# A decode step of sliding-window attention plus a gated MLP: sixteen rows of wq are loaded once more, first in SyncE's queue

## The chip, the cores and the metric

The kernel runs on one core of one Trainium2 chip. The metric is the device time of one execution in microseconds, as the median of several runs. The profile is of one execution, with the instructions of the engines (TensorE, VectorE, ScalarE, GpSimd, and SyncE, called SP, which here only issues DMAs) and the packets that the core's 16 DMA engines moved.

## The reference: what is computed

One token for each of two sequences (B = 2, D = 512) is normalised, and two branches are added to it: attention with 32 query heads and 8 key/value heads of size 128 over the last 4096 positions of a cache, and a gated MLP with F = 1792.

```python
xn = _layernorm(x)                                   # x: (2, 1, 512)
q  = (xn @ wq)                                       # wq: (512, 4096), 32 heads of 128
k, v = k_cache[:, :, -4096:, :], v_cache[:, :, -4096:, :]    # each head repeated for 4 query heads
p  = softmax(q k^T * 128 ** -0.5)
a  = (p v) @ wo                                      # wo: (4096, 512)
gate, up = xn @ W_gate, xn @ W_up                    # (512, 1792) each
b  = (gate * (gate > 0) * up) @ W_down               # (1792, 512)
return x + a + b
```

All numbers are float32. About 95 MB of weights and cache are read, each byte once, for very little arithmetic.

## The kernel before, in words

All large inputs pass through one SBUF tile, `ring`, of four slots of 128 partitions x 8192 floats (4 MB). `place` (line 74) hands out the slots in turn. wq takes two slots (64 KB for each partition), W_gate one, W_up one; then come the cache pieces (`load_kv`, line 98), one slot each, in four groups g of two k pieces and two v pieces; then W_down and the two halves of wo.

The DMAs are issued from two queues. ScalarE's (ACT) takes the loads of wq, W_gate and W_up (`load_rows`, line 79) at the very start, one behind the other and with no wait. SP's takes the input x in three pieces (line 121), and then all cache pieces, W_down (line 95) and wo (line 463), each of which waits until the slot that it writes has been read by TensorE or VectorE. Each DMA counts up one of eight counters (shown as DMAHW0 to DMAHW7), which are given out in turn.

The order in time is the order of the code: the schedule is written by hand. At the start GpSimd and VectorE make constants. VectorE waits for x, makes its statistics (line 187) and the normalised xn (line 204); TensorE turns it (line 208), VectorE copies it to `xnT` (line 213), and TensorE multiplies it with wq (line 221, `q_ps`). The heads are spread into `qz` (lines 229 to 250). Then come gate and up (line 258, `g_ps` and `u_ps`), their product `hh`, and `hT`.

Then each group g runs through `scores` (line 286), `maxima`, `softmax`, `turn`, `values` (line 351) and `gather`. In `scores` VectorE transposes a k piece in 32 x 32 blocks into tiles `kT` (line 294), which TensorE multiplies with `qz` (line 301). The kT tiles come from the pool `ktp`, which has three buffers of 128 partitions x 4096 floats, handed out in turn. The first kT tile is made once `hT` is written. At the end W_down and wo are multiplied with the hidden values and the heads (lines 438 to 445, tiles `y4` and `y_ps`), and ScalarE copies the sum and stores it (lines 476 and 477).

Of the kernel before, what the change touches and what calls it, by code (L numbers as in the profile page):

```python
# [9 lines left out]
F32 = mybir.dt.float32  # L10
# [10 lines left out]
def kernel(  # L21
# [12 lines left out]
    nc = tc.nc  # L34
    P = 128
# [5 lines left out]
    W = min(4096, max(256, SK // 4))  # L41
# [20 lines left out]
    ktp = ctx.enter_context(tc.tile_pool(name="ktp", bufs=3))  # L62
# [53 lines left out]
        return wo[r * rows:(r + 1) * rows, :].rearrange("(p j) e -> p j e", p=P)[:, j0:j1, :]  # L116


    x2 = const.tile([B, D], F32, name="x2")
    for c0, c1 in ((0, 256), (256, 384), (384, 512)):  # L120
        nc.sync.dma_start(x2[:, c0:c1], x[:, 0, c0:c1])
# [384 lines left out]
```

## Time and profile before

| | |
|---|---|
| median of 3 runs | 229.9 us (229.74 to 230.0) |
| span of the profiled execution (first to last instruction) | 228.1 us |
| median less span | 1.8 us |
| TensorE busy | 158.3 us (69%) |
| VectorE busy | 101.6 us (45%) |
| ScalarE, GpSimd busy | 8.6 us, 6.4 us |
| DMA, mean over the span | 95.03 MB at 417 GB/s |

For the profiled execution the profile holds the span; what lies outside it is not recorded, so its own time beyond the span is not known. In the rows of the timeline and of the groups, the number in brackets at the end is the time for which the engine sat idle before the instruction, and `<-` names what it waited for. SPq and ACTq are the sequencers that issue DMAs. A row of busy times by stretches has the stretch, its length, the busy time of PE, PEld (weight loads), VectorE, ScalarE and GpSimd with the number of instructions, the granted clock of TensorE, the busy share of the 16 DMA engines, and GB/s. There a packet is counted where it begins, with its whole length and bytes, so in a stretch shorter than a packet the share can be above 1 or 0.

### The profile page before, as it was taken

Reading aid. Unit: us, or ns where it says so; the run is one execution under the profiler, and the core shown is the slowest. Engines: PE = TensorE matmul, PEld = TensorE weight load, DVE = VectorE, ACT = ScalarE, POOL = GpSimd, SP = SyncE. Lnnn points to the kernel's source line nnn. Section 1 sums busy time; section 2 is a strip of 40 time slices with the busy share of each in tenths; the row PEclk is TensorE's granted clock in tenths of the full one; section 3 lists DMA queues with packets and bytes.
Section 4 is the critical chain, followed back from the end, with each engine's and each line's share of the span. In section 5 each row is a group of like instructions: output and inputs, shape, how many; then the busy total and the mean of one; then the engine's idle time right before and its main releaser. Section 6 shows DMA issues by size and latency. Waiting matters only on the chain.

```text
span 228.1 us, 2218 instructions
## 1 busy us (share of the span) xinstructions
PE 158.3 (69%) x952; PEld 52.2 (23%) x952; DVE 101.6 (45%) x120; ACT 8.6 (4%) x28; POOL 6.4 (3%) x24
## 2 busy tenths in 40 slices
PE   0011982937199767897857897857887785788974
PEld 0011231413022121222212221212241121122512
DVE  2040003212999312699722599922169972212000
ACT  0010012200000010000010000000000001000000
POOL 8100000000000000000000000000000000000000
PEclk9999997697559965999997999999999999589999
DMA  9898999999999999999999999999999999999991
GB/s 368 368 437 379 463 434 437 423 447 414 425 450 422 408 460 431 408 448 434 425 425 454 414 417 454 419 431 442 437 422 425 442 419 425 432 413 422 434 395 60
DMA packets 3784, 95.03 MB, mean 417 GB/s; under 512 B 430, under 2 KB 448, under 8 KB 704
## 3 DMA queue, kind: packets, MB, share of 16 engines
q1 hardware_dynamic: 3324, 79.17, 80.9%
q10 hardware_dynamic: 452, 15.74, 16.2%
q8 instruction: 7, 0.11, 0.2%
q14 instruction: 1, 0.01, 0.0%
HBM read 94.90 MB, written 0.00 MB: 416 GB/s over the span
## 4 chain that ended last, share of the span: by engine, by line
DMA 54%; DVE 23%; PE 16%; issue 5%; ACTq 1%; ACT 1%; DVEq 0%
DMA ring<-in_A_k_cache_dram 25%; DMA ring<-in_B_W_up_dram 21%; DVE kT L294 19%; DMA ring<-in_A_wo_dram 8%; PE o L358 4%; PE s L301 3%; PE pp L343 3%; PE u_ps L258 2%; PE y_ps L445 1%; DVE pt L345 1%; PE y L438 1%; DVE m L316 1%; DVE on L367 1%; PE ht_ps L274 0%; ACT p L337 0%
## 5 line engine op out<-in xcount | busy, mean ns | idle before, releaser
L294 DVE STREAM_TRANSPOSE kT<-ring 128x2048 f32<-128x2048 f32 x32 | 71.0, 2278 | 5.9 <-DMA ring<-in_A_k_cache_dram 5.9
L301 PE MATMUL s<-kT,qz 128*32 128x512 f32 x256 | 58.7, 635 | 14.8 <-DVE kT L294 14.7
L358 PE MATMUL o<-ring,pt 128*32 128x512 f32 x256 | 35.7, 658 | 4.8 <-DVE rl L349 4.8
L301 PEld LDWEIGHTS s<-kT,qz 128*32 128x32 f32 x256 | 13.8, 112 | 58.6 <-issue 34.0
L367 DVE TENSOR_TENSOR on<-o,mask 128x512 f32<-128x512 f32 x8 | 5.4, 680 | 23.1 <-PE o L358 23.1
L358 PEld LDWEIGHTS o<-ring,pt 128*32 128x32 f32 x256 | 10.0, 118 | 23.6 <-issue 18.4
L343 PE MATMUL pp<-p,perm 128*128 128x512 f32 x16 | 12.2, 908 | 4.5 <-ACT p L337 4.5
L208 PE MATMUL xt_ps<-rep,xn 2*128 2x32 f32 x8 | 2.0, 415 | 16.2 <-DVE xn L204 16.2
L221 PE MATMUL q_ps<-ring,xnT 128*32 128x512 f32 x64 | 9.0, 726 | 4.6 <-DMA ring<-in_A_wq_dram 4.6
L345 DVE STREAM_TRANSPOSE pt<-pp 128x1024 f32<-128x1024 f32 x4 | 5.0, 1250 | 16.0 <-PE pp L343 16.0
L373 PE MATMUL oa<-on,picks 128*16 128x512 f32 x16 | 8.3, 597 | 3.8 <-DVE on L367 3.8
L316 DVE TENSOR_REDUCE m<-s 128x1 f32<-128x512 f32 x4 | 2.8, 692 | 12.8 <-PE s L301 12.8
L337 ACT ACTIVATE p<-s,nm 128x512 f32<-128x512 f32 x4 | 2.7, 687 | 143.5 <-DVE nm L331 143.5
L258 PE MATMUL u_ps<-ring,xnT 128*32 128x448 f32 x32 | 4.9, 780 | 3.8 <-DMA ring<-in_B_W_up_dram 3.8
L236 DVE COPY qT<-qt 128x32 f32<-128x32 f32 x2 | 0.4, 192 | 15.2 <-PE qt L232 15.2
L248 DVE COPY qz<-rq 32x32 f32<-32x32 f32 x16 | 3.0, 187 | 7.1 <-ACT qz L248 7.1
L438 PE MATMUL y<-ring,oT 128*32 128x512 f32 x48 | 5.5, 594 | 0.8 <-DMA ring<-in_A_wo_dram 0.8
L309 PE MATMUL idle<-pt,ident 128*128 128x512 f32 x12 | 6.0, 618 | 0.0
L343 PEld LDWEIGHTS pp<-p,perm 128*128 128x128 f32 x16 | 3.8, 266 | 7.9 <-issue 4.3
L208 PEld LDWEIGHTS xt_ps<-rep,xn 2*128 2x128 f32 x8 | 1.9, 322 | 16.1 <-issue 16.1
L187 DVE BATCH_NORM_STATS2 stats<-x 2x6 f32<-2x512 f32 x1 | 0.7, 680 | 10.4 <-DMA x<-in_A_x_dram 10.4
L221 PEld LDWEIGHTS q_ps<-ring,xnT 128*32 128x32 f32 x64 | 2.5, 130 | 10.4 <-issue 10.4
(81 smaller groups left out, 73.9 us busy)
## 6 DMA issues: line engine op xcount, KB each, us to landing
ring<-in_A_k_cache_dram SPq DMA_DIRECT2D x8, 4096.0 KB, 22.2
ring<-in_A_v_cache_dram SPq DMA_DIRECT2D x8, 4096.0 KB, 22.2
ring<-in_A_wo_dram SPq DMA_DIRECT2D x3, 2048.0 KB
ring<-in_B_W_gate_dram ACTq DMA_DIRECT2D x1, 3584.0 KB, 30.0
ring<-in_B_W_up_dram ACTq DMA_DIRECT2D x1, 3584.0 KB
ring<-in_B_W_down_dram SPq DMA_DIRECT2D x1, 3584.0 KB, 28.8
ring<-in_A_wo_dram SPq DMA_DIRECT2D x1, 1280.0 KB, 20.1
ring<-in_A_wo_dram SPq DMA_DIRECT2D x1, 512.0 KB, 20.9
```

The costliest lines, as they stand in the source:

```text
L221: nc.tensor.matmul(q_ps[r][32 * c:32 * c + 32, :], xnT[:, kc, :], wqt[:, kc, n * 512:(n + 1) * 512], start=(kc == 0), stop=(kc == KC - 1),)
L258: nc.tensor.matmul(dst[32 * c:32 * c + 32, :], xnT[:, kc, :], wt[:, kc, c * MQ:(c + 1) * MQ], start=(kc == 0), stop=(kc == KC - 1),)
L294: nc.vector.transpose(kt[:, lo:lo + JH // 2].rearrange("p j c k h -> p (j c k h)"), kt_in[:, j * DH:(j + JH // 2) * DH],)
L301: nc.tensor.matmul(ss[g][lo:lo + 32, :], qz[:, g, cb, h, 16 * a:16 * a + 32], kt[:, :, cb, :, h], start=(a == 0 and cb == 0), stop=(a == N ...
L309: nc.tensor.matmul(idle, ident, pts[g][:, 2 * n:2 * n + 2].rearrange("p n j k -> p (n j k)"), start=True, stop=True)
L316: nc.vector.tensor_reduce(out=m, in_=ss[g], op=ALU.max, axis=AX.X)
L343: nc.tensor.matmul(pp[:, h], perm[:, h], p, start=True, stop=True)
L345: nc.vector.transpose(pts[g].rearrange("p n j k -> p j n k"), pp.rearrange("p h y -> p y h"))
L358: nc.tensor.matmul(o[32 * q:32 * q + 32, :], pts[g][:, a * S1 + s1, j:j + 4, :].rearrange("p u k -> p (u k)"), v[:, lo:lo + 512], start=(s ...
L367: nc.vector.tensor_tensor(ons[a], os[a].rearrange("p (u d) -> p u d", u=4), mask[:, :, None].to_broadcast([P, 4, P]), op=ALU.mult)
L373: nc.tensor.matmul(oa[g], picks[:, a].rearrange("p h a i -> p (h a i)"), ons[a], start=(a == 0), stop=(a == NP - 1))
L438: nc.tensor.matmul(y4[32 * t:32 * t + 32, :], lhsT.rearrange("p b s -> p (b s)"), w, start=(i < Q), stop=(i >= EARLY - Q))
```

## The change

Two lines are added ahead of the load of x. A tile `few` is taken from the pool of the kT tiles (its first buffer, which no other tile uses until the transposes begin), and SP issues a DMA that loads rows 0 to 15 of wq, 4096 floats (16 KB) each, into the partitions 0, 7, 14, ..., 105 of it. Nothing reads them. All else is as it was; the kT tiles begin with the second buffer of their pool, the line numbers after it move by two, and the counters of the later DMAs by one.

```diff
@@ -116,6 +116,8 @@
         return wo[r * rows:(r + 1) * rows, :].rearrange("(p j) e -> p j e", p=P)[:, j0:j1, :]
 
 
+    few = ktp.tile([P, P * W // 128], F32, name="few", tag="kT")
+    nc.sync.dma_start(few[0:16 * 7:7, :], wq[0:16, :])
     x2 = const.tile([B, D], F32, name="x2")
     for c0, c1 in ((0, 256), (256, 384), (384, 512)):
         nc.sync.dma_start(x2[:, c0:c1], x[:, 0, c0:c1])
```

SP's list of the kernel before begins with the three pieces of x (two have one shape and share a row), then the cache pieces, with the counters that each waits for:

```order
L121 DMA x_76<-in_A_x_dram 2x256
L121 DMA x_76<-in_A_x_dram 2x128 x2
L106 DMA ring<-in_A_k_cache_dram 128x1x8192 [waits DMAHW0_49,PE_49]
L106 DMA ring<-in_A_k_cache_dram 128x1x8192 [waits PE_49]
L106 DMA ring<-in_A_v_cache_dram 128x1x8192 [waits DMAHW4_49,PE_49]
```

Of the changed kernel it begins so:

```order
L120 DMA few<-in_A_wq_dram 16x4096
L123 DMA x_78<-in_A_x_dram 2x256
L123 DMA x_78<-in_A_x_dram 2x128 x2
L106 DMA ring<-in_A_k_cache_dram 128x1x8192 [waits DMAHW0_49,PE_49]
L106 DMA ring<-in_A_k_cache_dram 128x1x8192 [waits PE_49]
L106 DMA ring<-in_A_v_cache_dram 128x1x8192 [waits DMAHW5_49,DMAHW1_49,PE_49]
```

The load of few has no wait and stands ahead of x. W_gate's counter has moved from DMAHW4 to DMAHW5, and few has taken DMAHW1, which the first v load uses again and so waits for.

VectorE's first transposes, group 0 (kT_a_s is the tile of k piece a and half s), before:

```order
L294 STREAM_TRANSPOSE kT_0_0_309<-ring 128x2048 [waits DMAHW5_49,DMAHW0_49]
L294 STREAM_TRANSPOSE kT_0_0_309<-ring 128x2048
L294 STREAM_TRANSPOSE kT_0_1_320<-ring 128x2048 x2
L294 STREAM_TRANSPOSE kT_1_0_331<-ring 128x2048 [waits DMAHW7_49]
L294 STREAM_TRANSPOSE kT_1_0_331<-ring 128x2048
```

And of the changed kernel:

```order
L296 STREAM_TRANSPOSE kT_0_0_311<-ring 128x2048 [waits DMAHW6_49,DMAHW0_49]
L296 STREAM_TRANSPOSE kT_0_0_311<-ring 128x2048
L296 STREAM_TRANSPOSE kT_0_1_322<-ring 128x2048 x2
L296 STREAM_TRANSPOSE kT_1_0_333<-ring 128x2048 [waits DMAHW1_49,DMAHW0_49]
L296 STREAM_TRANSPOSE kT_1_0_333<-ring 128x2048
```

The third tile, kT_1_0, takes the buffer that few had and waits for few's counter besides that of its k piece.

## The prediction

> **What bounds the kernel now.** I read the page's part 2 and part 3 first: is the DMA ever idle?
>
> ```profile
> span 228.1 us, 2218 instructions
> DMA  9898999999999999999999999999999999999991
> q1 hardware_dynamic: 3324, 79.17, 80.9%
> q10 hardware_dynamic: 452, 15.74, 16.2%
> ```
>
> The 16 DMA engines are busy from the second slice to the last but one; q1 (SP's queue) and q10 (ACT's) together fill 97.1% of their span. The busy time by stretches shows the same (the last two columns are DMA share and GB/s):
>
> ```profile
> 1.50:22.50 21.00, 2.04 (x8) 1.94 (x8) 3.62 (x13) 1.28 (x1) 5.52 (x18) 1.00 1.00 422
> 22.50:49.50 27.00, 17.98 (x120) 7.49 (x120) 4.70 (x20) 3.93 (x18) 0.00 (x0) 0.87 1.00 429
> 49.50:97.00 47.50, 35.34 (x194) 10.54 (x198) 25.85 (x23) 0.78 (x2) 0.00 (x0) 0.75 1.00 432
> 97.00:195.00 98.00, 77.18 (x392) 23.09 (x385) 62.52 (x54) 2.33 (x6) 0.00 (x0) 0.98 1.00 431
> 195.00:221.00 26.00, 22.40 (x168) 7.48 (x170) 4.00 (x8) 0.00 (x0) 0.00 (x0) 0.89 0.99 421
> 224.00:228.00 4.00, 1.23 (x36) 0.48 (x24) 0.00 (x0) 0.27 (x1) 0.00 (x0) 1.00 0.02 6
> ```
>
> The share is 0.99 to 1.00 in every stretch up to 221 us, while PE is below it in each (77.18 of 98.00 us in the longest). So the end is the start of the stream plus its bytes over its rate, plus a short tail. Does the tail hang on the last byte? The timeline there says so:
>
> ```profile
> 222.97 2.25 PE L445 MATMUL y_ps<-ring,oT 128*17 128x128 f32 x64
> 224.81 0.13 PEld L445 LDWEIGHTS y_ps<-ring,oT 128*17 128x17 f32 x8 [0.28 <-DMA ring<-in_A_wo_dram]
> 225.29 0.27 ACT L476 COPY yo<-y_ps 128x128 f32<-128x128 f32 x1 [32.20 <-PE y_ps L445]
> ```
>
> The last matmuls of y_ps still wait for wo, and the copy and the store follow at once. Whatever lengthens the stream lengthens the kernel; a delay on another engine costs nothing unless it lets the stream run dry.
>
> **The change, part by part.** It adds one DMA of 16 x 16 KB = 262,144 bytes, first in SP's queue. Priced as stream at the 429 to 432 GB/s of the rows above, that is 262,144 / 431,000 = **0.61 us**, if it is spread evenly (16,384 bytes for each engine) and nothing hides it. But it runs at the start, so the question is whether the engines were doing anything useful then. The issues at the start (start, duration), then what the engines began in each small stretch:
>
> ```profile
> 0.74 0.39 ACTq L81 DMA_DIRECT2D ring<-in_A_wq_dram  x1
> 0.74 0.94 SPq L121 DMA_DIRECT2D x<-in_A_x_dram  x3
> ```
>
> ```profile
> 1.50:2.00 0.50, 0.00 (x0) 0.00 (x0) 0.50 (x3) 0.00 (x0) 0.50 (x1) 1.00 3.62 1184
> 2.00:2.50 0.50, 0.00 (x0) 0.00 (x0) 0.47 (x2) 0.00 (x0) 0.50 (x1) 1.00 1.51 524
> 2.50:3.00 0.50, 0.00 (x0) 0.00 (x0) 0.00 (x0) 0.00 (x0) 0.50 (x2) 1.00 0.91 393
> 4.00:4.80 0.80, 0.00 (x0) 0.00 (x0) 0.00 (x0) 0.00 (x0) 0.74 (x4) 1.00 0.00 0
> 4.80:5.00 0.20, 0.00 (x0) 0.00 (x0) 0.00 (x0) 0.00 (x0) 0.20 (x2) 1.00 4.54 1969
> 5.00:5.20 0.20, 0.00 (x0) 0.00 (x0) 0.00 (x0) 0.00 (x0) 0.14 (x2) 1.00 4.54 1969
> 5.20:5.50 0.30, 0.00 (x0) 0.00 (x0) 0.00 (x0) 0.00 (x0) 0.24 (x3) 1.00 2.02 874
> 7.00:8.00 1.00, 0.00 (x0) 0.00 (x0) 0.00 (x0) 0.00 (x0) 0.00 (x0) 1.00 2.42 1049
> ```
>
> A share above 1 is a packet counted whole where it begins. wq is 128 rows of 64 KB, eight for each engine, so these are rounds of one row per engine. The round at 7 us takes 2.42 us, the second (4.54 x 0.20 + 4.54 x 0.20 + 2.02 x 0.30) also 2.42. The first, however, takes (3.62 + 1.51 + 0.91) x 0.50 = 3.02: its packets begin between 1.5 and 3.0 us but last 0.60 us longer. Six engines begin their second row in 4.80 to 5.00, six in 5.00 to 5.20, four in 5.20 to 5.50: on average at 5.09. Less 2.42, the first row flowed, in effect, from 2.67 on (2.4 to 3.1 by engine). And x's first pieces, issued at the same 0.74, were through long before:
>
> ```profile
> DMA packets 3, 0.00 MB, mean 15 GB/s; under 512 B 1, under 2 KB 3, under 8 KB 3
> q1 hardware_dynamic: 3, 0.00, 4.3%
> ```
>
> That is the stretch 1.60 to 1.74: three small packets of SP's queue, already moved. So from about 1.67 to 2.67 an engine could carry SP's packets without taking time from wq. few's packet needs 0.61 and ends at 2.28 if it begins where x's did.
>
> The bounds: 0 if it fits on every engine; 0.61 if wq's first row waits behind it and pays its 0.60 all the same. Below nothing there is a little room: if the slow beginning falls on few instead and wq flows from 2.28 on, 0.39 us are gained. The nearest rows (x's packets, same queue, same moment) lie at the low end, but they are two rows on two engines, and few's sixteen have to be set out before wq's; I take a third of the full price, **+0.2 us**.
>
> Next, the waits. In SP's list few stands ahead of x, and the first v load now waits for few's counter (DMAHW1) besides W_gate's; on VectorE the third kT tile takes few's buffer and waits for it besides the cache load. Both wait for a transfer of the first microseconds at instructions that stand behind the k loads of 28.44 us (row below). They cost nothing, and nobody queued behind them waits longer.
>
> x is another matter. Packets of SP's queue in 4.80 to 5.20 and in 12.00 to 12.40:
>
> ```profile
> DMA packets 14, 0.79 MB, mean 1969 GB/s; under 512 B 0, under 2 KB 2, under 8 KB 2
> q1 hardware_dynamic: 2, 0.00, 0.8%
> DMA packets 11, 0.59 MB, mean 1475 GB/s; under 512 B 2, under 2 KB 2, under 8 KB 2
> q1 hardware_dynamic: 2, 0.00, 0.3%
> ```
>
> Two data pieces (512 B) at the first place, two tiny completion writes at the second, one per engine: SP's queue gets one packet in, then a whole 64 KB row of wq, then the next. x's second and third pieces need data and completion each: four turns, which is why x lands after the fourth row. few's data and completion stand ahead, so the eight packets of an engine are one before the first row and seven turns: three more (few's data lasts 0.61, and wq's row is there before it ends), 3 x 2.42 = 7.26 us, up to 7.87 with few's own 0.61. The rows that this pushes:
>
> ```profile
> 12.83 0.68 DVE L187 BATCH_NORM_STATS2 stats<-x 2x6 f32<-2x512 f32 x1 [10.35 <-DMA x<-in_A_x_dram]
> 18.25 0.29 DVE L213 COPY xnT<-xt_ps 128x128 f32<-128x128 f32 x1 [2.23 <-PE xt_ps L208]
> 22.80 2.79 PE L221 MATMUL q_ps<-ring,xnT 128*32 128x512 f32 x12 [4.59 <-DMA ring<-in_A_wq_dram]
> 28.44 3.97 SPq L106 DMA_DIRECT2D ring<-in_A_k_cache_dram  x2
> 49.60 4.91 PE L258 MATMUL u_ps<-ring,xnT 128*32 128x448 f32 x32 [3.80 <-DMA ring<-in_B_W_up_dram]
> 93.20 5.83 SPq L106 DMA_DIRECT2D ring<-in_A_v_cache_dram  x2
> ```
>
> xnT is ready at 18.54 now, and PE starts at 22.80 on wq: 4.2 us of cover. After, xnT comes at 25.8 to 26.4, so q's matmuls start 3.1 to 3.6 us late. **That is hidden twice.** PE idles 3.80 us before u_ps for W_up, so it catches up there; with k's first load issued later (28.44 plus 3.1 to 3.6) gate and up have the engines to themselves for longer and land earlier. Meanwhile the stream has gate and up queued. Without the 3.80 the next cover is the queue. The sizes of the loads:
>
> ```profile
> ring<-in_A_k_cache_dram SPq DMA_DIRECT2D x8, 4096.0 KB, 22.2
> ring<-in_B_W_gate_dram ACTq DMA_DIRECT2D x1, 3584.0 KB, 30.0
> ring<-in_B_W_up_dram ACTq DMA_DIRECT2D x1, 3584.0 KB
> ```
>
> The cover is then this: the nine loads ahead of the v load issued at 93.20 are 39,936 KB (wq 8192, gate and up 3584 each, six cache loads of 4096), which the stretches above have moved by 97.0 (21 x 422 + 27 x 429 + 47.5 x 432 = 40.96 MB), so 3.8 us of work is still queued then.
>
> [...]
>
> Sum: +0.2 (few at the start) + 0 (waits) + 0 (x late, covered). Profiled span 228.1 to 228.3. The median shown, 229.9, stands 1.8 us above that span; I leave these outside parts as they are: **230.1 us**.
>
> **The rivals.**
>
> Paid in full: few's packets and wq's first rows share whatever made the first round slow, so nothing is hidden and the stream moves by 0.61: 229.9 + 0.6 = 230.5, slower. For it: most engines began their first row together (3.62 of the 6.04 in the first half microsecond), so the loss may be a contention that few joins. It decides from the point where few ends later than 2.4 + 0.46 on the engine that finishes last. Against: x's packets passed freely at that moment. Chance 0.28.
>
> [...] Chance 0.05.
>
> The stream runs dry: PE is late by more than 3.80 + 3.8, less the 0.93 from an issue (0.74) to its first packet (1.67), that is 6.7 us. Two turns more than I count would give 7.9 to 8.4 and a gap of 1.2 to 1.7: 231.1 to 231.6. For it: turns are long. Against: wq has only eight rows per engine, so there are hardly turns left. Chance 0.03, with an uneven spread of few's rows over the engines in it.
>
> The slow beginning is absorbed: wq flows from 2.28, -0.39, 229.5; still within 0.2%, and beyond it only if more than the mean is won. Chance 0.04 for faster.
>
> **How the numbers follow.** A difference under 0.2% (0.46 us) can't be told from none. Forecast, and the cases beside it that stay within 0.46 us: 0.60. Slower: 0.28 + 0.05 + 0.03 = 0.36. Faster: 0.04. The range is 229.5 (absorbed) to 230.9 (paid in full with some of the spread between engines); the doubled door and the dry stream are left out.
>
> **What would show it.** In the changed profile: x lands three turns later (stats at about 20.1 to 20.7); q's matmuls start at 25.9 to 26.4, waiting for xnT and no longer for wq; u_ps no longer waits for W_up but starts within 0.5 us of 49.6; the DMA share stays at 0.99 or 1.00 up to 221 us. The deciding row is the second round of wq: if it begins at 5.1 to 5.3 on average few was hidden, if at 5.7 it was paid. I am wrong if that round moves by over 0.46, or if a gap in the DMA share appears near 97 us.

## The result and the profile after

The changed kernel takes 231.18 us (median of 4 runs, 231.07 to 231.33) against 229.82 us before (4 runs): **1.36 us slower**, a ratio of 1.0055 with a 95% interval of 1.0036 to 1.0074. The prediction said 230.1, at most 230.9, and no measurable change as the likeliest case.

The page of the changed kernel, the same rows as before:

```profile
span 229.3 us, 2220 instructions
DMA  9988999999999999999999999999999999999991
q1 hardware_dynamic: 3356, 79.44, 80.8%
q10 hardware_dynamic: 452, 15.74, 16.4%
```

q1 has 32 packets more: sixteen rows of few and sixteen completions. The span grew by 1.2 us. The stream is as full as it was, and the same stretches show it (the last two columns are DMA share and GB/s):

```profile
1.50:22.50 21.00, 0.00 (x0) 0.00 (x0) 0.97 (x4) 0.00 (x0) 4.97 (x17) 1.00 1.01 412
22.50:49.50 27.00, 16.67 (x100) 8.36 (x104) 5.30 (x21) 3.45 (x11) 0.55 (x1) 0.92 0.99 427
49.50:97.00 47.50, 35.03 (x232) 10.44 (x225) 29.41 (x33) 2.54 (x10) 0.00 (x0) 0.90 1.01 431
97.00:195.00 98.00, 77.51 (x381) 22.97 (x382) 61.05 (x53) 2.33 (x6) 0.00 (x0) 0.93 1.01 432
195.00:221.00 26.00, 22.48 (x157) 7.28 (x157) 4.00 (x8) 0.00 (x0) 0.00 (x0) 0.87 0.99 421
```

The share never falls, but the first stretch moves 412 GB/s in place of 422: the engines are as busy as before and move fewer bytes. All later stretches have the rate of before, within 2 GB/s. So the loss is in the first 22 us. Where? The same view of the start, by rounds of wq:

```profile
1.50:2.00 0.50, 0.00 (x0) 0.00 (x0) 0.50 (x3) 0.00 (x0) 0.50 (x1) 1.00 5.18 1704
2.00:2.50 0.50, 0.00 (x0) 0.00 (x0) 0.47 (x2) 0.00 (x0) 0.50 (x1) 1.00 1.17 393
4.50:5.50 1.00, 0.00 (x0) 0.00 (x0) 0.00 (x0) 0.00 (x0) 0.81 (x7) 1.00 2.42 1049
7.00:7.75 0.75, 0.00 (x0) 0.00 (x0) 0.00 (x0) 0.00 (x0) 0.00 (x0) 1.00 1.00 350
7.75:9.00 1.25, 0.00 (x0) 0.00 (x0) 0.00 (x0) 0.00 (x0) 0.00 (x0) 1.00 2.20 839
10.00:11.50 1.50, 0.00 (x0) 0.00 (x0) 0.00 (x0) 0.00 (x0) 0.00 (x0) 1.00 1.62 699
```

The first row of wq now begins by 2.5 us on all sixteen engines. Nothing of SP's queue is ahead of it: no packet begins in 1.60 to 1.74, where x's first pieces were before, and those that begin in 1.74 to 3.00 are all of ACT's queue:

```profile
DMA packets 16, 1.05 MB, mean 832 GB/s; under 512 B 0, under 2 KB 0, under 8 KB 0
q10 hardware_dynamic: 16, 1.05, 251.7%
```

The second row follows at 4.50 to 5.50 as before. Only then, at 7.00 to 7.75, comes something new. The packets that begin in 7.15 to 7.75:

```profile
DMA packets 16, 0.26 MB, mean 437 GB/s; under 512 B 0, under 2 KB 0, under 8 KB 0
q1 hardware_dynamic: 16, 0.26, 125.2%
```

That is few, sixteen packets of 16 KB. They take 1.252 x 0.60 = 0.75 us on average, not 0.61. And wq's third row, behind them, takes 2.20 x 1.25 = 2.75 us in place of 2.42; the fourth is back at 1.62 x 1.50 = 2.43. So few costs 0.75 + 0.33 = **1.08 us** of every engine: 0.61 of bytes and about 0.47 of something else (0.46 in the expectations below). The end has moved by as much (the copy of yo, 225.29 before):

```profile
226.34 0.27 ACT L478 COPY yo<-y_ps 128x128 f32<-128x128 f32 x1 [32.11 <-PE y_ps L447]
```

That is 1.05 us later; the store behind it adds 0.1 to the span, and what the median has beyond that (1.36 against 1.2) lies within the spread of the runs.

The other thing that the prediction followed, the late x:

```profile
0.74 0.63 SPq L120 DMA_DIRECT2D few<-in_A_wq_dram  x1
1.42 1.23 SPq L123 DMA_DIRECT2D x<-in_A_x_dram  x3
24.08 0.68 DVE L189 BATCH_NORM_STATS2 stats<-x 2x6 f32<-2x512 f32 x1 [21.61 <-DMA x<-in_A_x_dram]
29.86 1.08 PE L223 MATMUL q_ps<-ring,xnT 128*32 128x512 f32 x4 [0.38 <-DVE xnT L215]
53.66 3.18 PE L260 MATMUL u_ps<-ring,xnT 128*32 128x448 f32 x32
53.91 3.54 SPq L106 DMA_DIRECT2D ring<-in_A_v_cache_dram  x2
59.87 2.31 DVE L296 STREAM_TRANSPOSE kT<-ring 128x2048 f32<-128x2048 f32 x1
91.69 5.83 SPq L106 DMA_DIRECT2D ring<-in_A_v_cache_dram  x2
```

x is 11.25 us late, TensorE starts on wq 7.06 us late, and the first transpose 2.35 us late. Yet the v load that was issued at 93.20 is issued at 91.69 here, in an execution in which TensorE was granted a clock of 0.90 between 49.5 and 97 us, against 0.75 before.

### The profile page after: what moved, and what is told of

It is laid out like the page before. It is cut to its first block, busy times and chain, and to the rows that moved or that the text cites. A ratio compares the mean times of both kernels' runs of the same rounds, so it can differ in the third digit from the quotient of the medians.

```text
span 229.3 us, 2220 instructions
## 1 busy us (share of the span) xinstructions
PE 156.1 (68%) x952; PEld 51.2 (22%) x952; DVE 101.7 (44%) x120; ACT 8.6 (4%) x28; POOL 6.4 (3%) x24
## 4 chain that ended last, share of the span: by engine, by line
DMA 43%; DVE 23%; PE 16%; issue 13%; POOL 2%; ACT 1%; POOLq 0%; ACTq 0%; DVEq 0%
DMA ring<-in_A_k_cache_dram 34%; DVE kT L296 19%; DMA ring<-in_A_wo_dram 8%; PE q_ps L223 4%; PE s L303 3%; PE o L360 3%; PE pp L345 2%; PE y_ps L447 1%; DVE pt L347 1%; PE xt_ps L210 1%; PE y L440 1%; DVE m L318 1%; DVE on L369 1%; POOL qz L131 1%; ACT p L339 0%
## 5 line engine op out<-in xcount | busy, mean ns | idle before, releaser
L303 PE MATMUL s<-kT,qz 128*32 128x512 f32 x256 | 57.5, 624 | 14.9 <-DVE kT L296 14.9
L360 PE MATMUL o<-ring,pt 128*32 128x512 f32 x256 | 36.2, 666 | 4.8 <-DVE rl L351 4.8
L345 PE MATMUL pp<-p,perm 128*128 128x512 f32 x16 | 11.7, 873 | 4.5 <-ACT p L339 4.5
L223 PE MATMUL q_ps<-ring,xnT 128*32 128x512 f32 x64 | 9.7, 773 | 0.4 <-DVE xnT L215 0.4
L440 PE MATMUL y<-ring,hT 128*32 128x512 f32 x28 | 4.7, 598 | 0.0
L260 PE MATMUL g_ps<-ring,xnT 128*32 128x448 f32 x32 | 4.7, 754 | 0.0
```

Of the source, the lines that this page charges most:

```text
L223: nc.tensor.matmul(q_ps[r][32 * c:32 * c + 32, :], xnT[:, kc, :], wqt[:, kc, n * 512:(n + 1) * 512], start=(kc == 0), stop=(kc == KC - 1),)
L303: nc.tensor.matmul(ss[g][lo:lo + 32, :], qz[:, g, cb, h, 16 * a:16 * a + 32], kt[:, :, cb, :, h], start=(a == 0 and cb == 0), stop=(a == N ...
L345: nc.tensor.matmul(pp[:, h], perm[:, h], p, start=True, stop=True)
L360: nc.tensor.matmul(o[32 * q:32 * q + 32, :], pts[g][:, a * S1 + s1, j:j + 4, :].rearrange("p u k -> p (u k)"), v[:, lo:lo + 512], start=(s ...
L440: nc.tensor.matmul(y4[32 * t:32 * t + 32, :], lhsT.rearrange("p b s -> p (b s)"), w, start=(i < Q), stop=(i >= EARLY - Q))
```

## The experiments

The theory after the result, called W, was that the 0.47 us come from where few's rows are written: that the packets for sixteen rows at partitions 0, 7, ..., 105 and those of the other loads hold each other up. That was the author's estimate; the traces don't show which engine writes which partition. Its rivals: the read side (R), the break in wq's rounds (B), the late x (L), and a fixed price for one more DMA (F). Differences are medians against the kernel before in the same set of runs (229.77 to 229.87 us).

**few behind x** (e1_x_first): the two added lines moved below the loads of x.

```diff
     for c0, c1 in ((0, 256), (256, 384), (384, 512)):
         nc.sync.dma_start(x2[:, c0:c1], x[:, 0, c0:c1])
+    few = ktp.tile([P, P * W // 128], F32, name="few", tag="kT")
+    nc.sync.dma_start(few[0:16 * 7:7, :], wq[0:16, :])
```

> few's load stands behind the three pieces of x in SP's queue; all else as in the changed kernel. Theory W (the write side: few's sixteen rows go to partitions that other engines write, so they get in each other's way, and the stream loses about 0.46 us besides few's 0.61): nothing changes for the stream, +1.1 to +1.4 against the kernel before, with x landing at 12 to 13 us again and q's matmuls starting near 23 to 24. Rival L (the late x makes part of the loss): only the bytes remain, +0.5 to +0.7.

231.00 us, +1.17 (ratio 1.0053, 1.0036 to 1.0070). x is back in time:

```profile
13.36 0.68 DVE L189 BATCH_NORM_STATS2 stats<-x 2x6 f32<-2x512 f32 x1 [10.88 <-DMA x<-in_A_x_dram]
23.80 2.79 PE L223 MATMUL q_ps<-ring,xnT 128*32 128x512 f32 x12 [5.05 <-DMA ring<-in_A_wq_dram]
```

TensorE starts 6.06 us earlier than in the changed kernel and waits for wq again, and nearly all of the loss stays. L falls as the main cause; the 0.2 us between the two kernels lie within their intervals.

**Another place to write, at the start** (e2_step1): partitions 0 to 15.

```diff
-    nc.sync.dma_start(few[0:16 * 7:7, :], wq[0:16, :])
+    nc.sync.dma_start(few[0:16, :], wq[0:16, :])
```

> few's rows go to partitions 0 to 15 in place of every seventh. [...] Rivals R (the read side: the same rows of wq read beside wq's own load, or read 16 KB apart) and B (the break in wq's rounds of 64 KB rows): no difference by where it is written, +1.1 to +1.4.

231.53 us, +1.70 (1.0073, 1.0058 to 1.0088). That is 0.34 more than with every seventh, with intervals that overlap, and less than the author's estimate for W, +2.5 to +3.5. Nor is the pair clean: SP's issue took 0.37 us here, and few's sixteen packets began in 1.7 to 2.1 us, ahead of wq's first row (2.6 to 3.4). The runs in the middle of the stream repeat the question. But this is the case that the prediction had assumed, few where x's first pieces were, and it wasn't hidden: wq's second row begins in 6.4 to 6.6 us, 1.4 after the 5.09 of before.

**Other memory to read** (e3_other_source): sixteen rows of 16 KB from W_down.

```diff
-    nc.sync.dma_start(few[0:16 * 7:7, :], wq[0:16, :])
+    nc.sync.dma_start(few[0:16 * 7:7, :], w_down.rearrange("(a b) e -> a (b e)", b=8)[0:16, :])
```

> few reads sixteen rows of 16 KB of W_down, which nothing else reads then, in place of wq's rows; written to every seventh partition as in the changed kernel. Rival R in the form that the same memory is read twice at once: the loss goes, +0.5 to +0.7. Theory W and rival B: +1.1 to +1.4.

231.09 us, +1.26 (1.0053, 1.0038 to 1.0068). That wq is read twice at once is not the cause.

**In the middle of the stream** (e4_mid): x first, few behind the first two k pieces, where only SP's queue has work.

```diff
         kt_in = [load_kv(k_cache, g, a) for a in range(NP)]
+        if g == 0:
+            nc.sync.dma_start(few[0:16 * 7:7, :], wq[0:16, :])
```

> few is loaded behind the two k pieces of the first group, at 48 to 60 us, where only SP's queue has work; x is first in SP's queue again. Rival B (the break in wq's rounds at the start): the loss of 0.46 goes, +0.5 to +0.7. Theory W: it stays, +1.0 to +1.4, and few's packets or the ones beside them last longer than 0.61 us and 1.22 us.

231.48 us, +1.65 (1.0072, 1.0057 to 1.0087). B falls: far from wq's rounds the loss is larger, above W's range too. The stretch in which few runs, in the kernel before:

```profile
57.00:65.00 8.00, 2.92 (x8) 0.72 (x10) 7.96 (x7) 0.00 (x0) 0.00 (x0) 0.53 1.02 438
```

and in this one:

```profile
57.00:65.00 8.00, 2.92 (x8) 0.72 (x10) 7.96 (x7) 0.00 (x0) 0.00 (x0) 0.68 1.04 397
```

GB/s divided by the share is the rate of an engine while it is busy: 438 / 1.02 = 429 before, 397 / 1.04 = 382 here. 47 of 429 for 8.00 x 1.04 us is 0.91 us lost, and with 0.61 of bytes 1.52, close to the 1.65 measured. The next four runs change only this line.

**All partitions** (m1_mid_128), the same bytes in pieces of 2 KB:

```diff
-            nc.sync.dma_start(few[0:16 * 7:7, :], wq[0:16, :])
+            nc.sync.dma_start(few[:, 0:512], wq[0:16, :].rearrange("a (b f) -> (a b) f", b=8))
```

> Against the run with few behind the first k pieces (+1.6 us, of which 0.61 are bytes): the same 262,144 bytes of wq at the same place, written to all 128 partitions, 2 KB each. Theory W (the loss comes from where sixteen rows are written): the loss goes, +0.6 to +0.8. Rival R (the loss comes from reading these rows) and rival F (a DMA more in the stream costs so much by itself): +1.4 to +1.7.

230.62 us, +0.76 (1.0033, 1.0021 to 1.0045).

```profile
57.00:65.00 8.00, 5.86 (x18) 1.50 (x22) 8.00 (x4) 0.00 (x0) 0.00 (x0) 0.50 1.01 430
```

430 / 1.01 = 426 GB/s: the loss is gone, and the bytes remain. R and F fall: the same memory is read, by a DMA at the same place. The pieces are smaller too, 2 KB in place of 16 KB, so this run alone can't tell the size of the pieces from the place of writing; the runs below that change only the partitions can.

**Partitions 0 to 15** (m2_mid_step1): `few[0:16, :]`.

> The same place, the rows to partitions 0 to 15. Theory W: more loss than with every seventh, +2.0 to +4. Rivals R and F: as before, +1.4 to +1.7.

232.50 us, +2.64 (1.0115, 1.0100 to 1.0130).

```profile
57.00:65.00 8.00, 5.87 (x24) 1.54 (x26) 7.74 (x4) 0.00 (x0) 0.00 (x0) 0.66 1.02 307
```

307 / 1.02 = 301 GB/s. The same rows, read in the same way, cost 1 us more only for where they land.

**A quarter of the bytes** (m3_mid_4k): `few[0:16 * 7:7, 0:1024]` from `wq[0:16, 0:1024]`.

> The same place and partitions (every seventh), but only the first 4 KB of each row, a quarter of the bytes (0.15 us). Theory W: the loss falls with the bytes, to about a quarter of 0.9, in all +0.3 to +0.5. Rival F: the loss of about 0.9 stays, +0.9 to +1.2.

230.27 us, +0.41 (1.0015, 1.0006 to 1.0024). The bytes are 0.15 of it; the loss, about 0.26, is a quarter of the 1.04 that the whole rows have beyond their 0.61. That agrees with a loss that goes with the bytes, and F's +0.9 lies outside the interval (0.14 to 0.55 us).

**Every fourth partition** (m4_mid_step4): `few[0:16 * 4:4, :]`, partitions 0 to 60.

> The same place, the rows to every fourth partition, 0 to 60, so that only the lower half of the partitions is written. [...] Rivals R and F: no change, +1.4 to +1.7.

231.54 us, +1.68 (1.0069, 1.0052 to 1.0086), with a stretch of

```profile
57.00:65.00 8.00, 3.00 (x8) 0.72 (x10) 7.96 (x7) 0.00 (x0) 0.00 (x0) 0.51 1.03 393
```

393 / 1.03 = 382 GB/s, just as with every seventh. A miss for W, for which the author had estimated +1.8 to +2.5: only the lower half is written, and it is no worse. Taken alone, +1.68 is what R and F expected; it is m1_mid_128 and m2_mid_step1 that speak against them. So it isn't the number of partitions in a half that counts. Perhaps it is which partitions they are; the next pair asks for that with nothing else changed.

**Eight rows, on partitions 0 to 28 or on 64 to 92** (n1_mid_8own, n2_mid_8other), behind the first k pieces again. "Own" and "other" in the labels are the author's estimate of which engines write there, which no trace shows. Both load rows 0 to 7 of wq (131,072 bytes), one row into every fourth partition:

```diff
+            nc.sync.dma_start(few[0:32:4, :], wq[0:8, :])      (n1_mid_8own)
+            nc.sync.dma_start(few[64:96:4, :], wq[0:8, :])     (n2_mid_8other)
```

> Behind the first k pieces again, but only rows 0 to 7 of wq (131,072 bytes), to partitions 0, 4, ..., 28. [...] Theory W in the form that few partitions are crowded as such: some loss, +0.9 to +1.3.

> [...] Crowding form: the same as with partitions 0 to 28.

230.21 us, +0.34 (1.0016, 1.0006 to 1.0025), against 231.20 us, +1.33 (1.0055, 1.0036 to 1.0075). The stretch of the first:

```profile
57.00:65.00 8.00, 5.96 (x24) 1.54 (x26) 8.00 (x4) 0.00 (x0) 0.00 (x0) 0.70 1.03 442
```

and of the second:

```profile
57.00:65.00 8.00, 3.08 (x8) 0.72 (x10) 7.97 (x6) 0.00 (x0) 0.00 (x0) 0.66 1.01 389
```

442 / 1.03 = 429 GB/s, no loss at all; 389 / 1.01 = 385, as much loss as from sixteen rows. As many rows, the same memory, the same distances: 64 partitions further up they cost 1 us more. The +0.34 is below the +0.9 to +1.3 for crowding, and below the +0.5 to +0.7 that the author had estimated for no loss; it is about what 131,072 bytes take of a stream of 431 GB/s, 0.30 us.

The packets in the traces say the same. few's eight take 0.61 us each on partitions 0 to 28, and 0.84 on average (0.65 to 1.05) on 64 to 92. The 32 KB packets of k that begin in 58 to 59 us last 1.21 to 1.22 us in the first run and 1.69 to 1.85 in the second. Between 52 and 66 us each packet begins within 6 ns of the end of another, so they can be followed engine by engine: in the second run all sixteen engines lose more than 0.7 us, the eight that carry no row of few as much as the eight that do.

**The start, all partitions** (s1_start_128): e1_x_first with the destination of m1_mid_128.

> Back at the start: x first, then the 262,144 bytes of wq to all 128 partitions, 2 KB each, in SP's queue beside wq's load. Theory W: the loss of 0.46 that the sixteen rows had there goes too, +0.6 to +0.8. Rival B (the break in wq's rounds adds its own loss): +1.0 to +1.4.

230.64 us, +0.77 (1.0033, 1.0022 to 1.0044): 0.4 us less than e1_x_first. wq's third row, beside few, lasts 2.42 us on average here and 2.84 there. So at the start, too, the loss goes when the same bytes are written to all partitions.

**ACT issues few ahead of wq** (s2_act_first): e1_x_first with `nc.scalar.dma_start`, every seventh partition.

> The sixteen rows to every seventh partition, but issued by ACT ahead of wq, so that they are the first packets of the engines; x alone ahead in SP's queue. The prediction's step that the first microsecond hides them: 0 to +0.4, with wq's second round beginning at 5.1 to 5.4 us. Theory W without hiding: +1.0 to +1.5, second round at 6.1 to 6.6.

230.89 us, +1.02 (1.0043, 1.0026 to 1.0060). Its second round of wq:

```profile
5.00:5.80 0.80, 0.00 (x0) 0.00 (x0) 0.14 (x1) 0.00 (x0) 0.67 (x6) 1.00 0.38 164
5.80:6.10 0.30, 0.00 (x0) 0.00 (x0) 0.00 (x0) 0.00 (x0) 0.24 (x2) 1.00 3.53 1529
6.10:6.50 0.40, 0.00 (x0) 0.00 (x0) 0.00 (x0) 0.00 (x0) 0.40 (x3) 1.00 2.65 1147
```

It begins near 6.05 (two of sixteen before 5.80, seven each in the other two), 0.95 later than before: not hidden. But hiding and the loss are mixed here.

**The same with all partitions** (t1_act_128): few issued by ACT ahead of wq, 2 KB to each of the 128 partitions.

> [...] If the first microsecond has room for SP's or ACT's first bytes, as the prediction had it: 0 to +0.4. If there is none: the bytes are paid, +0.6 to +0.8, and wq's second round begins 0.6 us later than the 5.1 of before.

230.34 us, +0.57 (1.0024, 1.0014 to 1.0034). Its second round:

```profile
5.30:5.60 0.30, 0.00 (x0) 0.00 (x0) 0.00 (x0) 0.00 (x0) 0.24 (x4) 1.00 5.56 2406
5.60:6.00 0.40, 0.00 (x0) 0.00 (x0) 0.00 (x0) 0.00 (x0) 0.40 (x3) 1.00 1.89 819
```

Eleven engines begin it in 5.30 to 5.60 and five after, near 5.54 on average, 0.44 after the 5.09 of before: a part of the bytes may have fitted into the first microsecond, and most were paid. The total doesn't tell the two apart: the interval of 0.3 to 0.8 us holds both the 0.61 of the bytes and 0.4.

**few first in SP's queue, eight rows on partitions 0 to 28** (t2_sp_8own): the changed kernel with the line of n1_mid_8own.

> [...] x is late as in the changed kernel. If the late x costs nothing: +0.2 to +0.6, as the same rows behind the k pieces (+0.34). If it costs: +0.7 or more.

230.42 us, +0.65 (1.0036, 1.0021 to 1.0051). The packets that begin in 7.05 to 7.65:

```profile
q10 hardware_dynamic: 8, 0.52, 201.6%
q1 hardware_dynamic: 8, 0.13, 50.9%
```

few's eight take 0.509 x 0.60 x 16 / 8 = 0.61 us each, and wq's eight rows beside them 2.016 x 0.60 x 16 / 8 = 2.42: no loss, at the very place where the changed kernel's took 0.75 and 2.75. The expectation had +0.2 to +0.6 for a late x that costs nothing, and +0.65 is 0.05 outside; it is also what the eight engines were given (0.61). Why n1_mid_8own, with the same rows, shows only +0.34 stayed open. No clean number for the late x follows, beyond that it is small.

## Why the prediction was wrong

**The bound** was right: the stream stayed full (a DMA share of 0.99 to 1.01 in every stretch of the changed kernel up to 221 us, and of 1.01 to 1.07 in 57 to 65 us where few stands behind the k pieces), and a later end of the stream is a later end of the kernel (yo 1.05 later for 1.08 at the start).

**The price of the bytes**, 0.61, was nearly right: where the loss is away the totals are +0.77 (s1_start_128), +0.76 (m1_mid_128) and +0.57 (t1_act_128), all in pieces of 2 KB.

**"few's packet needs 0.61 and ends at 2.28 if it begins where x's did"** is the step that failed, and with it the third of the price that was taken (+0.2, where every engine lost 1.08). In the changed profile no packet of SP's queue is ahead of wq, and few came after two rows of wq, from 7.2 us on, when nothing was free. Where SP's issue of few took 0.63, 0.62 and 0.81 us (the changed kernel, e3_other_source, t2_sp_8own) few came after two rows, and where it took 0.37 (e2_step1) it came first; that the length of the issue decides is an estimate from these four runs, and none changes it alone. And the first microsecond did not hide few where it was first: the second row of wq was 1.4 us late in e2_step1 and, without the loss from the place of writing, 0.44 in t1_act_128, so most of the 0.61 was paid.

The row that was to decide, wq's second, would have said the wrong thing: it begins at 5.07 on average in the changed kernel, "hidden" by the prediction's rule, because few came only behind it. Where a transfer lands in the order has to be known before one asks what it pushes.

**"0.61 if wq's first row waits behind it"** as the upper bound was the second fault: the loss of 0.47 us from where the rows are written had no place in the sum. Nor does any run show the term of 0.05 in the sum of the chances, the "doubled door" that the range leaves out: it was the author's estimate. What the runs show in its place is that eight rows, four partitions apart, lose nothing on partitions 0 to 28 (+0.34 in all, at 429 GB/s) and about 1 us on 64 to 92 (+1.33, at 385 GB/s), and that the packets of the other loads beside few's are stretched (wq's third row, 2.75 in place of 2.42). m4_mid_step4, with sixteen rows on partitions 0 to 60, has 382 GB/s, close to the 385 of the eight on 64 to 92. That the place of writing makes the loss is shown: +0.34 against +1.33 with eight rows, +1.65 against +2.64 with sixteen. How it makes it is not: that engines meet in writing was the author's estimate, for the traces don't number the engine that moved a packet, and it can't be the whole account: in n2_mid_8other the eight engines with few's rows lose on their own k packets behind them too (all sixteen lose more than 0.7 us). Why all sixteen engines lose about the same, whether the still larger loss on the first sixteen partitions has the same cause, and why the loss is larger in the middle (0.9 against 0.47), stayed open.

**x late, covered**: the outcome held, the numbers did not. x came 11.25 us later, not 7.3 to 7.9, since x's last piece landed behind eight rows of wq, where it had been four before and the prediction had counted seven, and few came between them; TensorE was 7.06 us late, not 3.1 to 3.6. That is above the 6.7 at which the stream was to run dry, yet the share stayed full: u_ps began 4.06 us late, no longer waiting for W_up, and ran in 3.18 us in place of 4.91, and the first transpose was 2.35 late. The faster u_ps is the clock's doing: TensorE was granted 1.00 in 53.66 to 56.84 us, and 0.57 in 50.5 to 54.5 before (0.65 over the whole of u_ps, 49.6 to 54.5, and 4.91 x 0.65 = 3.19). These 1.73 us of cover weren't in the prediction, so that the stream stayed full was in part luck, though u_ps took 3.18 in all four runs with few ahead of x. Behind it nothing ran dry: by the v load at 91.69 the delay was gone in the changed kernel, and in e3_other_source, with a clock of 0.75 between 49.5 and 97 us as before, that load was issued at 95.44, 2.24 late, and the DMA share in 93 to 100 us was 1.04. e1_x_first, with x in time, keeps 1.17 of the 1.36.

**The two added waits** cost nothing, as said; neither of the instructions waits for few in the changed profile.

## What to carry to other kernels

In a kernel whose DMA engines never rest, a small transfer can cost more than its bytes, by where it is written: here 0.61 us of bytes on sixteen scattered partitions cost 1.08 at the start, and 1.65 in the middle of the stream. The same bytes in pieces over all 128 partitions cost 0.77 and 0.76, and eight rows on partitions 0 to 28 in the middle +0.34, about their bytes (0.30). And a queue's order is not the order in which bytes move: few, first in SP's queue with an issue of 0.63 us, began at 7.2 us, behind two rows of wq from ACT's. Ask how long the issue takes and what the other queue has put on the engines by then.

## What had not been expected of the hardware

- Where sixteen rows of 16 KB were written changed the total by 1 us with nothing else changed: +1.65 on every seventh partition, +1.68 on every fourth, +2.64 on the first sixteen. The same bytes on all 128, in pieces of 2 KB, cost +0.76.
- Eight rows on partitions 64 to 92 cost +1.33, on 0 to 28 +0.34.
- The issue of few by SP at the start took 0.63 us for every seventh partition and 0.37 for the first sixteen (e2_step1), and few came behind two rows of wq in the one and ahead of them in the other. ACT's issue of the 128 rows of wq took 0.39 to 0.42 us beside them.
